# Stage C of a Fourier mix in products of 64 rows

## The chip, the cores and the metric

The kernel runs on one core of one Trainium2 chip. The metric is the time of one execution on the device in microseconds, as a median over several runs. TensorE multiplies, ScalarE (ACT) and VectorE (DVE) evacuate and combine, GpSimd (POOL) issues the loads, and SyncE (SP) issues most of the stores.

## The reference

The input `x` has 8 batches of 3072 rows and 256 columns. First the real part of a two-dimensional Fourier transform is taken, over the rows and the columns of each batch. Then follows a channel mix:

```
X = fft(fft(x, axis=1), axis=2).real
x_prev = X shifted by one row, zeros in front
xk = mu_k * X + (1 - mu_k) * x_prev
xr = mu_r * X + (1 - mu_r) * x_prev
k  = relu(xk @ w_k)              # 256 -> 1024
v  = (k * k) @ w_v               # 1024 -> 256
out = sigmoid(xr @ w_r) * v
```

## The kernel before

**Stages.** The transform of one batch goes through three stages of products on TensorE. Stage A (`a_item`, for the first two batches in part `a_sum`) transforms along one part of the row index. Stage D (`d_item`, L502) transforms the 256 columns and leaves its result in `g_all`: 13 units `u` of 256 columns on 128 partitions, the lower 64 of which belong to one value of the remaining row index and the upper 64 to another. `turned` (L524) corrects one column of each unit by a small product of 13 columns. Stage C (`c_item`, L527 to L543) finishes the row transform, for 27 slots of 64 rows of the result. For slot `sl` the weights are a unit `u` of `g_all`, of the first 128 columns (`f` = 0, giving p) or the second (`f` = 1, giving q), and the moving operand is `m_cs[:, f, sl]`, 64 columns. An odd slot needs only the lower 64 partitions of its unit and an even slot only the upper 64; `m_cs` has zeros in the other half, so that one product over all 128 partitions and 128 columns computes two neighbouring slots (192 columns and three slots for the first, which shares its unit). The products of an item go to one PSUM buffer, p in its first bank and q in the second, and ScalarE copies both to the tile `pq` (`evac`, L443). `halves` (L547 to L557) then forms p + q and p - q on VectorE into `y`; `diff`, `scaled` and `mixed` make the differences of neighbouring rows and the two mixed inputs out of it.

**Channel mix.** The rows of a batch are six chunks of 512. For each chunk there are four steps. In each, `k_piece` makes four products of 512 columns (L625) into a PSUM buffer, ScalarE takes the Relu (L635), and VectorE squares it later (L642). `v_tile` multiplies the squares of an earlier chunk with `w_v` in eight products of 256 columns (L663), five steps behind. Once for each chunk `r_item` makes eight products of 256 columns (L649), and ScalarE takes their sigmoid.

**Order.** The order of all work is written out by hand. A step is: `k_piece`, then the items that the dictionary `work` holds for the step as kind "x" (stages A, D and C, `turned`, `r_item`), then `v_tile`, then kind "w" (VectorE's parts and the loads), then the output and the squares. A batch has 24 steps, and while batch b is mixed, batches b+1 and b+2 go through the transform. Stage C of batch t = b+2 stands at steps 24b+35, 37, 39 and 41 (that is, 11, 13, 15 and 17 of the next batch), with 7, 8, 6 and 6 slots; that of batch 1 at steps 16 to 19. `halves` of a batch stands at steps 16 and 18 of the batch before it (17 and 20 for batch 1). `pin_order` keeps each engine's instructions in the order in which they are written.

**PSUM.** The large buffers (`ps_w`, 1024 columns of float32, two banks) are three in rotation; `k_piece`, the "x" items and `r_item` share them. Two small ones (`ps_v`) serve `v_tile`. A product that takes a buffer waits until its last reader is done.

Batch 0's stage C uses `c_item` in smaller pieces, some of them with an extra product one column wide (`turn_late`), and is not changed but for the layout of `pq`.

Of the kernel before, what the change touches and what calls it, by code (L numbers as in the profile page):

```python
# [10 lines left out]
FP16 = mybir.dt.float16  # L11
# [9 lines left out]
def _v(ap, extra_offset, free_dims):  # L21
    new_ap = [list(ap.ap[0])] + [[s, c] for (s, c) in free_dims]
    return dataclasses.replace(ap, offset=ap.offset + extra_offset, ap=new_ap)
# [16 lines left out]
def kernel(  # L40
# [10 lines left out]
    nc = tc.nc  # L51
# [3 lines left out]
    P = 128  # L55
    N1, R = 48, 64
    NSL = 27
    NU = 26
    NJ, NJ1, NJ2 = 14, 6, 9
# [5 lines left out]
    y_pool = ctx.enter_context(tc.tile_pool(name="y_sb", bufs=1))  # L65
# [8 lines left out]
    def ps_slot(kind, n, cols):  # L74
        k = ps_n[kind] % n
        ps_n[kind] += 1
        return psum.tile([P, cols], FP32, name=f"ps{kind}{k}", tag=f"ps{kind}{k}", bufs=1)

    def ps_w():
        return ps_slot("W", 3, 1024)  # L80

    def ps_v():
        return ps_slot("V", 2, 512)
# [23 lines left out]
    V = nc.vector  # L107
# [122 lines left out]
    g_all = const.tile([P, NU // 2, 256], FP16)  # L230
# [3 lines left out]
    m_cs = const.tile([P, 2, 2 * NJ, 64], FP16)  # L234
# [125 lines left out]
    ps = ps_v()  # L360
    for a in range(2):
        nc.tensor.matmul(out=ps[:, 2 * a:2 * a + 2], lhsT=mu_p[:, a], rhs=unit, start=True,
                         stop=True)
# [73 lines left out]
    y_t = {}  # L437

    def evac(out_ap, in_ap, eng):
        if eng == "V":  # L440
            V.tensor_copy(out=out_ap, in_=in_ap)
        else:
            nc.scalar.activation(out=out_ap, in_=in_ap, func=AF.Copy)  # L443
# [83 lines left out]
    def c_item(b, s0, n, eng="A", turn_late=False, small=False):  # L527

        if s0 == 0:
            y_t[b] = y_pool.tile([P, 2, NSL, 64], FP16, name="y")  # L530
            y_t[b, "pq"] = y_pool.tile([P, 2, NSL, 64], FP16, name="pq")
        pq = y_t[b, "pq"]
        ps, bank = (ps_v(), 256) if small else (ps_w(), 512)
        cuts = [s0] + list(range(s0 + (1 + s0 % 2 if s0 else 3), s0 + n, 2))
        for f in range(3 if turn_late else 2):
            for sl in cuts:
                k = min(1 + sl % 2 if sl else 3, s0 + n - sl)
                o, u = bank * min(f, 1) + 64 * (sl - s0), max(sl - 1, 0) // 2
                m = 1 if f == 2 else P
                nc.tensor.matmul(out=ps[0:m, o:o + 64 * k],  # L540
                                 lhsT=g_all[:, u, 128 * min(f, 1):128 * min(f, 1) + m],
                                 rhs=m_cs[:, f % 2, sl:sl + k], start=True, stop=True)
        evac(pq[:, :, s0:s0 + n, :], _v(ps, 0, [(bank, 2), (64, n), (1, 64)]), eng)  # L543


    x_t = {}
# [1 line left out]
    def halves(b, lo, hi, hs=(0, 1)):  # L548

        pq = y_t[b, "pq"]  # L550
        if b and (lo, hs[0]) == (0, 0):

            V.tensor_scalar(out=pq[0:1, 1, 0], in0=pq[0:1, 1, 0], scalar1=-1.0, scalar2=None,
                            op0=ALU.mult)
        for h in hs:
            V.tensor_tensor(out=y_t[b][:, h, lo:hi], in0=pq[:, 0, lo:hi], in1=pq[:, 1, lo:hi],  # L556
                            op=ALU.subtract if h else ALU.add)  # L557

    def diff(b, lo, hi, hs=(0, 1)):
# [150 lines left out]
    ps = ps_w()  # L710
    for u, eng in ((4, "A"), (6, "V")):
        d_half(0, u, ps[:, 256 * u - 1024:256 * u - 512], eng)
    c_item(0, 0, 5, "A", True)
    c_item(0, 5, 4, "A", True)
    c_item(0, 9, 4, "A", True, True)
    c_item(0, 13, 4, "A", True, True)

    work = {}  # L720

    def at(step, f, *args):
        work.setdefault((step, "x" if f in (a_item, a_sum, d_item, c_item, turned, r_item) else "w"),
                        []).append((f, args))

    def mirrored_mu():
# [12 lines left out]
    for step, (c, tb) in v_steps.items():  # L739
        if c == chunks[-1] and tb >= 2:  # L740
            o_steps[step] = [(c, tb, 1)]
        elif tb % 2:
            o_steps[step + (step == LAG)] = [(c, tb, 2)]
    halves(0, 0, 5)
    diff(0, 0, 4)
    mix_part(0, 0, 0, 4)
    halves(0, 5, 9)
    keep_busy(20, ps_w(), 128)
    k_products(chunks[0], 0, 0, 256)
# [3 lines left out]
    for n, c in enumerate(chunks):  # L753
        at(4 * n + (4, 5, 6)[(n < 3) + (n == 0)], r_item, c)


    at(0, halves, 0, 9, 17)
    at(0, diff, 0, 8, 16)
    at(0, mix_part, 0, 0, 8, 16)
    at(4, loads_2)  # L760
# [30 lines left out]
    for n, st0 in enumerate((11, 12, 13, 14)):  # L791
        at(st0, d_item, 1, n)
    at(15, turned, 0, 13)
    for n, st0 in enumerate((16, 17, 18, 19)):
        at(st0, c_item, 1, (0, 7, 15, 21)[n], (7, 8, 6, 6)[n])

    for b in range(B):
        s0 = 24 * b

        for n, st0 in enumerate((2, 4, 6, 8) if b else ()):  # L800
            at(s0 + st0, mix, b, n // 2, 1, n % 2)
        if b + 3 < B:
            for h in range(2):
                at(s0 + 12 + 2 * h, load_xh, b + 3, h)
        t = b + 2
        if t < B:
            for n, st0 in enumerate((9, 10, 12, 14) if b else (13, 15, 16, 24)):
                at(s0 + st0, butterfly if n % 2 else fold, t, n // 2)
            for n, st0 in enumerate((18, 21, 23, 25) if b else (18, 21, 25, 26)):
                at(s0 + st0, a_item, t, n // 2, n % 2)  # L810
            for n, st0 in enumerate((27, 29, 31, 33)):
                at(s0 + st0, d_item, t, n)
            at(s0 + 34, turned, 0, 13)
            for n, st0 in enumerate((35, 37, 39, 41)):
                at(s0 + st0, c_item, t, (0, 7, 15, 21)[n], (7, 8, 6, 6)[n])
        t = b + 1
        if t < B:
            at(s0 + (16 if b else 17), halves, t, 0, 15)
            at(s0 + (18 if b else 20), halves, t, 15, 27)
            at(s0 + (19 if b else 20), diff, t, 0, 26, (0,))  # L820
            at(s0 + (20 if b else 22), diff, t, 0, 26, (1,))
            at(s0 + 21, mix, t, 0, 0, 0)
            at(s0 + 22, mix, t, 0, 0, 1)
            at(s0 + 24, mix, t, 1, 0, 0)
            at(s0 + 25, mix, t, 1, 0, 1)
# [51 lines left out]
```

## Time and profile before

| | |
|---|---|
| median of 3 runs | 444.59 us (444.22 to 444.69) |
| the profiled execution | 443.51 us, span 441.7 us |
| granted clock of TensorE | 1.00 |
| TensorE busy | 431.9 us, 98% |
| VectorE busy | 361.0 us, 82% |
| ScalarE busy | 326.7 us, 74% |
| stage C's products (L540) | 216, of which 34 in batch 0 |

Lines of the profile name a source line, an engine, an operation and the tiles: `PE L540 MATMUL psW<-m_cs,g_all 128*128 128x128 f16 x8` are eight products at L540, with weights of 128 rows and 128 columns (128*128) and a moving operand of 128 rows and 128 columns. PE are the products, PEld the weight loads, each of which is an instruction of its own. In a timeline the first number is the start and the second the time covered, in us from the start of the span; neighbouring instructions of one kind are merged. Products are pipelined: a product lasts longer than the distance to the next one, and that distance is what it costs.

### The profile page before, as it was taken

Reading aid. Unit: us, or ns where it says so; the run is one execution under the profiler, and the core shown is the slowest. Engines: PE = TensorE matmul, PEld = TensorE weight load, DVE = VectorE, ACT = ScalarE, POOL = GpSimd, SP = SyncE. Lnnn points to the kernel's source line nnn. Section 1 sums busy time; section 2 is a strip of 40 time slices with the busy share of each in tenths; the row PEclk is TensorE's granted clock in tenths of the full one; section 3 lists DMA queues with packets and bytes.
Section 4 is the critical chain, followed back from the end, with each engine's and each line's share of the span. In section 5 each row is a group of like instructions: output and inputs, shape, how many; then the busy total and the mean of one; then the engine's idle time right before and its main releaser. Section 6 shows DMA issues by size and latency. Waiting matters only on the chain.

```text
span 441.7 us, 8525 instructions
## 1 busy us (share of the span) xinstructions
PE 431.9 (98%) x3484; PEld 309.4 (70%) x3484; DVE 361.0 (82%) x532; ACT 326.7 (74%) x377; POOL 50.9 (12%) x66
## 2 busy tenths in 40 slices
PE   9889999999999999999999999999999999999995
PEld 3657776777777777777777777777777777676764
DVE  7699999988798978978799887989789756997553
ACT  8669887877777777787777777777777877666661
POOL 7763030004000120002200010000000000000000
PEclk9999999999999999999999999999999999999999
DMA  7998676239523492326723273232322223233334
GB/s 126 182 207 129 134 132 140 57 68 162 128 53 73 77 193 61 64 60 114 171 48 73 54 138 71 51 73 48 73 60 62 63 57 72 49 73 72 73 73 95
DMA packets 34507, 40.93 MB, mean 93 GB/s; under 512 B 3906, under 2 KB 30788, under 8 KB 34468
## 3 DMA queue, kind: packets, MB, share of 16 engines
q1 hardware_dynamic: 27524, 25.05, 25.3%
q0 software_dynamic: 6784, 15.21, 21.3%
q8 instruction: 27, 0.44, 0.4%
q10 hardware_dynamic: 160, 0.13, 0.1%
q14 instruction: 12, 0.10, 0.1%
HBM read 30.41 MB, written 25.17 MB: 126 GB/s over the span
## 4 chain that ended last, share of the span: by engine, by line
PE 86%; DVE 5%; DMA 4%; POOL 2%; issue 1%; ACT 1%; POOLq 0%
PE psV L663 36%; PE psW L625 35%; PE psW L649 9%; DMA xp<-in_x_dram 2%; PE psW L502 2%; PE psW L540 2%; PE psW L463 2%; DMA wr<-in_moe_w_r_dram,row_i 2%; DVE k L642 1%; POOL xm L125 1%; DVE x L589 1%; POOL wk L125 1%; DVE d L564 1%; DVE p L153 1%; DVE t L576 1%
## 5 line engine op out<-in xcount | busy, mean ns | idle before, releaser
L635 ACT ACTIVATE rl<-psW 128x1024 f16<-128x1024 f32 x192 | 196.4, 1024 | 101.5 <-PE psW L625 97.6
L663 PE MATMUL psV<-wv_sb,k 128*128 128x256 f16 x1536 | 198.9, 273 | 0.3 <-DVE k L642 0.3
L625 PE MATMUL psW<-x,wk 128*128 128x512 f16 (+1 forms) x776 | 197.3, 377 | 1.9 <-ACT rl L635 0.8
L663 PEld LDWEIGHTS <-k 128*128 128x128 f16 x1536 | 146.1, 98 | 28.5 <-DVE k L642 0.6
L642 DVE TENSOR_TENSOR k<-rl 128x2048 f16<-128x2048 f16 (+1 forms) x98 | 117.6, 1201 | 50.5 <-ACT rl L635 50.2
L625 PEld LDWEIGHTS <-wk 128*128 128x128 f16 x776 | 75.9, 98 | 52.1 <-issue 2.8
L673 DVE SCALAR_TENSOR_TENSOR o<-psV,r 128x512 f32<-128x512 f32 (+1 forms) x97 | 66.1, 682 | 16.1 <-PE psV L663 13.7
L589 DVE TENSOR_TENSOR x<-y,t 128x1536 f16<-128x1536 f16 (+1 forms) x70 | 61.8, 882 | 2.4
L649 PE MATMUL psW<-wr,x 128*128 128x256 f16 x384 | 49.8, 273 | 0.0
L654 ACT ACTIVATE r<-psW 128x1024 f16<-128x1024 f32 x48 | 48.9, 1018 | 0.8 <-PE psW L649 0.8
L649 PEld LDWEIGHTS <-x 128*128 128x128 f16 x384 | 37.6, 98 | 14.6 <-issue 0.3
L125 POOL DMA_INDIRECT xm<-in_x_dram,idx x25 | 31.3, 1250 | 8.1 <-issue 6.9
L122 POOL DMA_DIRECT2D xp<-in_x_dram x16 | 9.1, 567 | 192.6 <-DVE p L155 184.5
L443 ACT ACTIVATE pq<-psW 128x768 f16<-128x768 f32 (+5 forms) x32 | 27.4, 858 | 1.0 <-PE psW L540 1.0
L443 ACT ACTIVATE g_all<-psW 128x1024 f16<-128x1024 f32 (+4 forms) x39 | 27.7, 712 | 0.0
L443 ACT ACTIVATE a<-psW 128x832 f16<-128x832 f32 x30 | 25.8, 859 | 1.8 <-PE psW L480 1.8
L153 DVE TENSOR_TENSOR p<-xp,xm 96x2304 f16<-96x2304 f16 (+3 forms) x19 | 20.9, 1101 | 0.0
L576 DVE TENSOR_SCALAR t<-d,mu_f 128x1536 f16<-128x1536 f16 (+1 forms) x38 | 20.6, 542 | 0.1
L540 PEld LDWEIGHTS <-g_all 128*128 128x128 f16 (+1 forms) x216 | 14.9, 97 | 7.7
L502 PEld LDWEIGHTS <-a 128*128 128x128 f16 x208 | 14.1, 98 | 8.2 <-issue 1.2
L576 DVE TENSOR_SCALAR t<-d,mu_m 128x1536 f16<-128x1536 f16 x32 | 19.7, 615 | 0.0
L556 DVE TENSOR_TENSOR y<-pq 128x960 f16<-128x960 f16 (+5 forms) x38 | 18.6, 532 | 1.0 <-ACT pq L443 0.8
(99 smaller groups left out, 182.7 us busy)
## 6 DMA issues: line engine op xcount, KB each, us to landing
out_dram<-o SPq DMA_DIRECT2D x190, 128.0 KB, 2.4
xp<-in_x_dram POOLq DMA_DIRECT2D x8, 432.0 KB, 6.6
xp<-in_x_dram POOLq DMA_DIRECT2D x8, 384.0 KB, 4.7
wv_sb<-in_moe_w_v_dram POOLq DMA_DIRECT2D x1, 512.0 KB, 8.3
xm<-in_x_dram,idx POOLq DMA_INDIRECT x25, 7.3
out_dram<-o ACTq DMA_DIRECT2D x2, 64.0 KB, 2.1
out_dram<-o SPq DMA_DIRECT2D x2, 64.0 KB, 2.2
wk<-in_moe_w_k_dram,row_i POOLq DMA_INDIRECT x4, 7.1
```

The source lines that it names most:

```text
L125: nc.gpsimd.indirect_dma_start(dst, None, src, bass.IndirectOffsetOnAxis(ap=idx, axis=0))
L153: V.tensor_tensor(out=p[:, q0:q0 + n], in0=xp[:, q0:q0 + n], in1=_v(xm, o + 256, [(-256, n), (-1, 256)]), op=ALU.add)
L443: nc.scalar.activation(out=out_ap, in_=in_ap, func=AF.Copy)
L576: V.tensor_scalar(out=dst, in0=src, scalar1=mu, scalar2=None, op0=ALU.mult)
L589: V.tensor_tensor(out=dst, in0=_v(y_t[b], 64 * (NSL * a + lo + 3 * m), [(1, n)]), in1=_v(x_t["t", a], 64 * lo, [(1, n)]), op=ALU.subtract ...
L625: nc.tensor.matmul(out=st["k", ds][:, 512 * hs + lo:512 * hs + hi], lhsT=wk_sb[m][a][:, 128 * fc:128 * fc + 128], rhs=xk[:, a, 512 * i + l ...
L635: nc.scalar.activation(out=st["rl"][:, 2 * ds:2 * ds + 2], in_=st["k", ds].rearrange("p (f t) -> p f t", f=2), func=AF.Relu, bias=0.0, sca ...
L642: V.tensor_tensor(out=k2_t[c][:, lo:hi], in0=r, in1=r, op=ALU.mult)
L649: nc.tensor.matmul(out=ps[:, 256 * tb:256 * tb + 256], lhsT=x_t[b, 1, m][:, a, 512 * i + 128 * tb: 512 * i + 128 * tb + 128], rhs=wr_sb[m] ...
L654: nc.scalar.activation(out=st["r", c], in_=ps, func=AF.Sigmoid)
L663: nc.tensor.matmul(out=st["v", tb - h][:, 256 * h:256 * h + 256], lhsT=k2_t[c][:, fc, 128 * tb:128 * tb + 128], rhs=wv_sb[:, fc], start=(f ...
L673: V.scalar_tensor_tensor(out=o.rearrange("p a b -> p (a b)")[:, 0:256 * n], in0=st["v", t0][:, 0:256 * n], scalar=16.0, in1=st["r", c][:, ...
```

## The change

Stage C of batches 1 to 7 goes through a new function, `c_pairs`. For each slot it uses only the 64 partitions that the slot needs: rows 0 to 63 of `g_all` and `m_cs` for an odd slot, rows 64 to 127 for an even one. Every slot is then two products of 64 rows, 64 moving columns and 128 weight columns (p and q), each with its own weight load. The products alternate between an odd and an even slot, and the two write to different banks of the PSUM buffer. 28 slots are computed, one more than is used. The items are four of 8, 8, 8 and 4 slots, two and two in one step: steps 16, 16, 19, 19 for batch 1, and 24b+36, 36, 39, 39 for the others. The tile `pq` is laid out by slot and then p or q, so that an evacuation writes runs of 128 elements, and `halves` reads runs of 64 with gaps of 64.

```diff
         if s0 == 0:
             y_t[b] = y_pool.tile([P, 2, NSL, 64], FP16, name="y")
-            y_t[b, "pq"] = y_pool.tile([P, 2, NSL, 64], FP16, name="pq")
+            y_t[b, "pq"] = y_pool.tile([P, 2 * NJ, 2, 64], FP16, name="pq")
...
-        evac(pq[:, :, s0:s0 + n, :], _v(ps, 0, [(bank, 2), (64, n), (1, 64)]), eng)
+        evac(_v(pq, 128 * s0, [(64, 2), (128, n), (1, 64)]),
+             _v(ps, 0, [(bank, 2), (64, n), (1, 64)]), eng)
+
+    def c_pairs(b, s0, n):
+        if s0 == 0:
+            y_t[b] = y_pool.tile([P, 2, NSL, 64], FP16, name="y")
+            y_t[b, "pq"] = y_pool.tile([P, 2 * NJ, 2, 64], FP16, name="pq")
+        ps = ps_w()
+        for i in range(n // 2):
+            for f in range(2):
+                for odd in (1, 0):
+                    sl = s0 + 2 * i + odd
+                    o, u = 512 * odd + 128 * i + 64 * f, min(max(sl - 1, 0) // 2, NU // 2 - 1)
+                    rows = slice(0, 64) if odd else slice(64, 128)
+                    nc.tensor.matmul(out=ps[:, o:o + 64],
+                                     lhsT=g_all[rows, u, 128 * f:128 * f + 128],
+                                     rhs=m_cs[rows, f, sl], start=True, stop=True)
+        evac(_v(y_t[b, "pq"], 128 * s0, [(256, n // 2), (128, 2), (1, 128)]),
+             _v(ps, 0, [(128, n // 2), (512, 2), (1, 128)]), "A")
...
-            V.tensor_scalar(out=pq[0:1, 1, 0], in0=pq[0:1, 1, 0], scalar1=-1.0, scalar2=None,
+            V.tensor_scalar(out=pq[0:1, 0, 1], in0=pq[0:1, 0, 1], scalar1=-1.0, scalar2=None,
                             op0=ALU.mult)
         for h in hs:
-            V.tensor_tensor(out=y_t[b][:, h, lo:hi], in0=pq[:, 0, lo:hi], in1=pq[:, 1, lo:hi],
+            V.tensor_tensor(out=y_t[b][:, h, lo:hi], in0=pq[:, lo:hi, 0], in1=pq[:, lo:hi, 1],
                             op=ALU.subtract if h else ALU.add)
...
-        work.setdefault((step, "x" if f in (a_item, a_sum, d_item, c_item, turned, r_item) else "w"),
+        work.setdefault((step, "x" if f in (a_item, a_sum, d_item, c_item, c_pairs, turned, r_item) else "w"),
                         []).append((f, args))
...
-    for n, st0 in enumerate((16, 17, 18, 19)):
-        at(st0, c_item, 1, (0, 7, 15, 21)[n], (7, 8, 6, 6)[n])
+    for n, st0 in enumerate((16, 16, 19, 19)):
+        at(st0, c_pairs, 1, 8 * n, (8, 8, 8, 4)[n])
...
-            for n, st0 in enumerate((35, 37, 39, 41)):
-                at(s0 + st0, c_item, t, (0, 7, 15, 21)[n], (7, 8, 6, 6)[n])
+            for n, st0 in enumerate((36, 36, 39, 39)):
+                at(s0 + st0, c_pairs, t, 8 * n, (8, 8, 8, 4)[n])
```

## The prediction

> **What bounds the kernel now.** I read the page's busy line first, then the chain that ended last, then the timeline of one stretch of the steady state, and last the timeline where TensorE changes between shapes of different height or width.
>
> ```profile
> PE 431.9 (98%) x3484; PEld 309.4 (70%) x3484; DVE 361.0 (82%) x532; ACT 326.7 (74%) x377; POOL 50.9 (12%) x66
> ...
> PE 86%; DVE 5%; DMA 4%; POOL 2%; issue 1%; ACT 1%; POOLq 0%
> ...
> L540 PEld LDWEIGHTS <-g_all 128*128 128x128 f16 (+1 forms) x216 | 14.9, 97 | 7.7
> ```
>
> TensorE is busy for 98% of the span and is 86% of the chain; stage C (L540) is a small part of it. The timeline says what a product costs when the next one follows at once (ACT's lines in it are used further on):
>
> ```profile
> 151.27 0.19 PE L524 MATMUL psW<-g_all,turn 128*128 128x13 f16 x1
> 151.30 1.03 PE L663 MATMUL psV<-wv_sb,k 128*128 128x256 f16 x8
> ...
> 153.03 0.55 PE L540 MATMUL psW<-m_cs,g_all 128*128 128x192 f16 x6
> ...
> 153.42 1.04 PE L663 MATMUL psV<-wv_sb,k 128*128 128x256 f16 x8
> ...
> 154.29 1.03 PE L625 MATMUL psW<-x,wk 128*128 128x512 f16 x4
> ...
> 155.16 1.04 PE L649 MATMUL psW<-wr,x 128*128 128x256 f16 x8
> 155.36 1.02 ACT L635 ACTIVATE rl<-psW 128x1024 f16<-128x1024 f32 x1 [0.29 <-PE psW L625]
> ...
> 156.90 1.03 PE L625 MATMUL psW<-x,wk 128*128 128x512 f16 x4
> ...
> 157.77 0.61 PE L540 MATMUL psW<-m_cs,g_all 128*128 128x128 f16 x8
> ...
> 158.21 1.04 PE L663 MATMUL psV<-wv_sb,k 128*128 128x256 f16 x8
> ```
>
> Starts, not durations, are to be read. Four products of 512 columns take 156.90 to 157.77, 217 ns each; eight of 128 take 157.77 to 158.21, 55 ns each. Each has a weight load of its own, and it is hidden. The straight line through the two sizes is 0.42 ns a column and gives 28 ns for 64 columns. The product of 13 columns took 30 ns (151.27 to 151.30), where the line says 7. So a product and its load, on the same rows, do not follow closer than some 30 ns.
>
> Entering and leaving another tile shape is in two views of the start, products first, weight loads second:
>
> ```profile
> 25.53 0.27 PE L625 MATMUL psW<-x,wk 128*128 128x256 f16 x1
> 25.73 0.17 PE L301 MATMUL psW<-rw 1*128 1x1 f16 x1
> ```
> ```profile
> 25.42 0.10 PEld L625 LDWEIGHTS <-wk 128*128 128x128 f16 x1
> 25.73 0.11 PEld L301 LDWEIGHTS <-rw 1*128 1x128 f16 x2 [0.21 <-issue]
> 25.86 0.10 PEld L625 LDWEIGHTS <-wk 128*128 128x128 f16 x1
> ```
>
> A 256-column product is followed after 0.11 us elsewhere (153.42 to 154.29 for eight). Before a product of one row it takes 0.20 us (25.53 to 25.73), and the load is not pulled ahead: 0.09 us more. On the way back, the second one-row product began at about 25.77 (the two end at 25.93, and one lasts 0.16), and the next load of full height at 25.86, 0.09 us later against some 0.03: 0.06 us more. The same drain stands at a change of width:
>
> ```profile
> 20.65 0.22 PE L540 MATMUL psW<-m_cs,g_all 128*1 128x128 f16 x1
> 20.80 0.29 PE L540 MATMUL psV<-m_cs,g_all 128*128 128x128 f16 x2
> ```
>
> A product of 128 columns, then 0.15 us to the next start where 55 ns is usual: 0.095 us more.
>
> **The change, part by part.**
>
> *Removed.* Stage C of one batch is 26 products of 128 rows in four items. By the timeline, the first item takes 153.03 to 153.42 and the second 157.77 to 158.21; the two of six products take 6 x 55 ns each. 0.39 + 0.44 + 0.33 + 0.33 = 1.49 us for a batch.
>
> *Added products.* 28 slots in two products each are 56 products of 64 columns, every one with its own load. No row shows two products on different halves of the rows side by side. By the nearest rows on each side, 28 ns (line) and 30 ns (13 columns), I take 29 ns: 56 x 29 = 1.62 us, 0.13 us more than before. Bound below: the halves overlap fully and a pair takes 29 ns, 0.81 us, 0.68 us less. Bound above: in this mode a load is no longer hidden by the product before it, 28 + 29 = 57 ns each, 3.19 us, 1.70 us more. I take the middle because every row has a load in each spacing, and none goes under that floor.
>
> *Added changes of height.* The items stand two and two in a step, so TensorE goes to 64 rows and back twice in a batch. Each group costs 0.09 in and 0.06 to 0.095 out, 0.15 to 0.19; two are 0.30 to 0.38, and I take 0.35 us. Nothing covers it, since TensorE is the bound; it would be nothing only if 64 rows counted as the same shape as 128, as 96 rows do (L463 follows L625 without a gap).
>
> *Sum for a batch:* 0.13 + 0.35 = +0.48 us on TensorE.
>
> *Which batches pay.* The seven behind the first are changed. For batches 2 to 7 TensorE runs without a gap around stage C, so 6 x 0.48 = 2.9 us reach the end. Batch 1 is different: its halves, differences and mixes (L556 to L589) end late on VectorE, and TensorE waits for them:
>
> ```profile
> 75.88 0.96 DVE L589 TENSOR_TENSOR x<-y,t 128x1536 f16<-128x1536 f16 x1
> 76.04 0.38 PE L625 MATMUL psW<-x,wk 128*128 128x512 f16 x1
> ...
> 76.89 0.81 PE L625 MATMUL psW<-x,wk 128*128 128x512 f16 x3 [0.47 <-DVE x L589]
> ```
>
> From 76.04 the next product is due at 76.26 and starts at 76.89: 0.63 us of slack. An extra 0.48 us is swallowed there if VectorE's chain stays where it is. Batch 1 counts 0, between -0.3 (its last halves come earlier) and +0.48.
>
> *Evacuations.* ScalarE now copies 1024 + 1024 + 1024 + 512 columns instead of 896 + 1024 + 768 + 768. By the page's rows, 3 x 1.02 + 0.59 = 3.65 us instead of 0.91 + 1.02 + 0.81 + 0.81 = 3.55. ScalarE idles for a quarter of the span, so the 0.1 us is hidden. What is new is their place: two in one step, behind the Relu and, in the first of the two steps, a Sigmoid. Let T be the start of that step's 512-column products. The second item takes the PSUM buffer of that step's own Relu. The stretch from 154.29 has the Relu start 1.07 us after T (155.36) and end at T + 2.09. The K products end their turn at T + 0.87, R's at T + 1.74, the drain makes it 1.83, and the first item's 16 products end at T + 2.30. So the buffer is free 0.2 us early. ScalarE then works to T + 5.15, the next Relu starts some 0.35 us late, and nobody needs it soon: its products are used by V five steps after the chunk began. The second step has no Sigmoid and room left. Cost 0; if the products overlapped, the buffer would be 0.05 us late.
>
> *VectorE.* The halves now read p and q in runs of 64 with gaps. Nearest row: the butterfly reads runs of 128 with gaps and takes 680 ns for 1024 elements, against 685 for the contiguous square of 1024. I take 0. The other end is the rate of the copy out of PSUM, 691 ns for 512 (1.35 ns an element instead of 0.7): some 2.2 us a batch, hidden by VectorE's idle 18%, but for batch 1 it would lie on the path. No DMA is moved or passed; the halves keep their steps, and what they wait for is ready one or two steps earlier.
>
> **Sum.** The profiled execution took 443.51 us (span 441.7), 1.08 below the median of 444.59. 443.51 + 2.9 = 446.4 us; on the median, 447.5 us. Own range of this case: 28 ns and 0.30 give +2.3, seven batches at 30 ns and 0.38 give +4.0, so 446.9 to 448.6.
>
> **The rivals.**
>
> *The halves overlap (faster).* If the load and the product on one half run beside those on the other, a pair takes 29 ns, and a batch 0.81 + 0.35 - 1.49 = -0.33 us. Six batches give -2.0, and seven -2.3: 442.3 to 442.6; with the late buffer 442.8. I give 442.6. It decides below 41 ns a pair, since 28 x 41 + 350 ns is 1.49 us. Against it: no two starts with loads in the trace are closer than some 30 ns. For it: in all those rows load and product share their rows, so the floor may belong to one set of rows and not to the queue. By the Trainium skill, "TensorE: Matmul & The Clock Gate", part 3 on packing small matmuls, products on different row groups start some 4 ns apart, and a load overlaps a product in flight where the row group differs; that is this rival, and no run so far shows it.
>
> *Half an overlap.* A pair of 38 to 45 ns leaves a batch within 0.12 us of before: 444 to 445.4. No row speaks for it.
>
> *Loads exposed.* 57 ns for every product: +1.70 + 0.35 = 2.05 us a batch, 7 x 2.05 - 0.63 = +13.7, 458 us. For it: after a change of shape the load was not pulled ahead. Against it: the two one-row loads began 0.02 us apart (0.11 us for two of 0.09). If the loads are exposed but the halves overlap, a pair takes 57 ns, which is the forecast again.
>
> *The change does nothing on the path* would need TensorE to have slack at stage C; of the late batches none has.
>
> **How the numbers follow.** Forecast 0.50, halves overlap 0.36, half an overlap 0.06, loads exposed 0.08. A measurement tells about 0.2% (0.9 us) from no change. Faster: 0.37 (overlap, and a little of the half). Same: 0.06. Slower: 0.57. The range 442.3 to 448.6 takes in forecast and overlap; outside are the exposed loads and an overlap that is better than 29 ns a pair.
>
> **What would show it.** Right: starts of the 64-column products some 29 ns apart, or in twos 57 ns apart; 0.09 us before the first and after the last of each group; the gap at 76 us shorter by some 0.5 us. Wrong: pairs that follow after 30 ns, groups without a gap at their ends, the L556 rows longer, or TensorE waiting for a Relu in the second item.

## The result and the profile after

The changed kernel takes 442.86 us (median, 442.19 to 443.21), the one before 444.22 us (seven runs of each): a ratio of 0.9968, with a 95% interval of 0.9956 to 0.9980. It is faster by 1.36 us, where 3 us slower was forecast. In two later comparisons it came out at 0.9968 (0.9946 to 0.9990) and 0.9970 (0.9960 to 0.9981).

The busy line of the page after, and the chain:

```profile
PE 430.6 (98%) x3694; PEld 304.8 (69%) x3694; DVE 360.4 (82%) x532; ACT 326.1 (74%) x377; POOL 48.5 (11%) x66
...
PE 90%; DVE 6%; ACT 1%; DMA 1%; issue 1%
```

TensorE is the bound as before and is busy 1.3 us less, with 210 more products. The timeline of TensorE at the two groups of one batch shows where that comes from:

```profile
154.42 1.04 PE L670 MATMUL psW<-wr,x 128*128 128x256 f16 x8
155.39 0.72 PE L560 MATMUL psW<-m_cs,g_all 64*128 64x64 f16 x32
156.03 0.61 PE L684 MATMUL psV<-wv_sb,k 128*128 128x256 f16 x4
```
```profile
160.82 0.59 PE L646 MATMUL psW<-x,wk 128*128 128x512 f16 x2
161.35 0.52 PE L560 MATMUL psW<-m_cs,g_all 64*128 64x64 f16 x24
161.81 0.39 PE L684 MATMUL psV<-wv_sb,k 128*128 128x256 f16 x2
```

Read the starts. 24 products of 64 columns and their way out take 161.35 to 161.81, 0.46 us, or 19 ns each with everything in it. At 29 ns each the products alone would have taken 0.70 us. A window that ends some 15 ns into the first group has two products in it, which together last as long as one:

```profile
155.39 0.20 PE L560 MATMUL psW<-m_cs,g_all 64*128 64x64 f16 x2
```

Start by start, the trace gives this for the second group (ns from one start to the next):

```
4 35 3 26 3 26 3 26 4 25 4 26 3 26 3 26 3 26 3 26 4 25 4
```

Two products start 3 to 4 ns apart, and the next two 29 ns after them. The weight loads come in twos in the same way, 3 to 4 ns apart. The two halves run side by side, loads included. By the Trainium skill, "TensorE: Matmul & The Clock Gate", part 3, products on different row groups start some 4 ns apart; the trace agrees, with 3 to 4. In the second item of the first group, which starts behind a wait, the two of a pair start 6 to 20 ns apart, and still two come in every 29 ns.

The changes of height are there too. From the last 256-column product to the first of 64 rows it is 205 ns instead of 109, and from a 512-column one 311 instead of 216 (0.095 us more). From the last of 64 rows to the next product it is 122 ns instead of 29 (0.093 us more), and that next product itself is followed after 120 ns instead of 109 (0.011 us more). In the first group there is a third loss: 89 ns instead of 26 between the two items. ScalarE's timeline names it:

```profile
154.62 1.02 ACT L656 ACTIVATE rl<-psW 128x1024 f16<-128x1024 f32 x1 [0.71 <-PE psW L646]
155.54 1.02 ACT L675 ACTIVATE r<-psW 128x1024 f16<-128x1024 f32 x1
```

The Relu ends at 155.64, and the second item, which takes its PSUM buffer, begins at 155.69.

From the product before a group to the product after it, less what the product before takes itself, the groups cost 0.744 and 0.551 us in every batch; with the 0.011 us behind each they come to 1.317 us together. Before, stage C cost 1.505 us, measured in the same way. That is 0.19 us less a batch. The distance from `turned` in one batch to `turned` in the next says the same: 51.28 us instead of 51.47 for every batch from the second on. For batches 2 to 7 it makes 1.12 us. Batch 1 has the gap in front of it:

```profile
75.71 0.96 DVE L610 TENSOR_TENSOR x<-y,t 128x1536 f16<-128x1536 f16 x1
...
75.83 0.38 PE L646 MATMUL psW<-x,wk 128*128 128x512 f16 x1
...
76.72 0.59 PE L646 MATMUL psW<-x,wk 128*128 128x512 f16 x2 [0.51 <-DVE x L610]
```

TensorE arrives 0.21 us earlier (75.83, before 76.04) and goes on 0.17 us earlier (76.72, before 76.89), since VectorE's mix ends earlier. 1.12 + 0.17 = 1.29 us, which is the difference of the two spans (441.7 and 440.4 us); the medians differ by 1.36. VectorE's halves cost what they did:

```profile
L577 DVE TENSOR_TENSOR y<-pq 128x960 f16<-128x960 f16 x14 | 8.6, 656 | 0.3
...
L577 DVE TENSOR_TENSOR y<-pq 128x768 f16<-128x768 f16 x14 | 7.2, 553 | 0.2 <-ACT pq L443 0.2
```

656 and 553 ns stand against 655 and 552 before: runs of 64 with gaps cost next to nothing.

### The profile page after: what moved, and what is told of

It is laid out like the page before. It is cut to its first block, busy times and chain, and to the rows that moved or that the text cites. A ratio compares the mean times of both kernels' runs of the same rounds, so it can differ in the third digit from the quotient of the medians.

```text
span 440.4 us, 8945 instructions
## 1 busy us (share of the span) xinstructions
PE 430.6 (98%) x3694; PEld 304.8 (69%) x3694; DVE 360.4 (82%) x532; ACT 326.1 (74%) x377; POOL 48.5 (11%) x66
## 4 chain that ended last, share of the span: by engine, by line
PE 90%; DVE 6%; ACT 1%; DMA 1%; issue 1%
PE psV L684 37%; PE psW L646 35%; PE psW L670 9%; PE psW L502 2%; PE psW L463 2%; PE psW L185 2%; PE psW L560 2%; DVE k L663 1%; DMA xp<-in_x_dram 1%; DVE d L585 1%; DVE x L610 1%; DVE p L153 1%; DVE t L597 1%; PE psV L301 1%; DVE y L577 1%
## 5 line engine op out<-in xcount | busy, mean ns | idle before, releaser
L646 PE MATMUL psW<-x,wk 128*128 128x512 f16 (+1 forms) x776 | 197.3, 377 | 1.9 <-ACT rl L656 0.8
L646 PEld LDWEIGHTS <-wk 128*128 128x128 f16 x776 | 75.9, 98 | 52.1 <-issue 2.8
L125 POOL DMA_INDIRECT xm<-in_x_dram,idx x25 | 28.5, 1140 | 8.1 <-issue 6.9
L443 ACT ACTIVATE pq<-psW 128x1024 f16<-128x1024 f32 (+3 forms) x32 | 26.8, 892 | 1.0 <-PE psW L540 1.0
L163 DVE TENSOR_TENSOR eo<-p 96x1024 f16<-96x1024 f16 (+2 forms) x28 | 17.8, 676 | 0.0
```

What stands on the lines that cost most here:

```text
L125: nc.gpsimd.indirect_dma_start(dst, None, src, bass.IndirectOffsetOnAxis(ap=idx, axis=0))
L646: nc.tensor.matmul(out=st["k", ds][:, 512 * hs + lo:512 * hs + hi], lhsT=wk_sb[m][a][:, 128 * fc:128 * fc + 128], rhs=xk[:, a, 512 * i + l ...
```

## The experiments

The theory after the result: loads and products of one half run beside those of the other, and each half by itself keeps the 29 ns of before. The rivals: a product of 64 rows is cheaper in any order; or the gain lies in the steps and the evacuations. The first four of these kernels ran on one chip.

**Neighbours on the same half.**

```diff
-        for i in range(n // 2):
-            for f in range(2):
-                for odd in (1, 0):
+        for odd in (1, 0):
+            for i in range(n // 2):
+                for f in range(2):
...
```

> The changed kernel, but within each item all products of the lower 64 rows come first and then all of the upper 64, so neighbours share a half. Theory (a load and a product on one half run beside those on the other half, and each half by itself keeps the old floor of some 29 ns): starts 28 to 30 ns apart, 56 x 29 = 1.64 us a batch, plus 0.38 for four changes of height, less the 1.50 of before: +0.5 us a batch, six batches count, +3.1 us on the kernel before, ratio 1.007. Rival (a product of 64 rows is itself cheaper, in whatever order, for instance because a load of half the height takes half the time): starts some 15 ns apart as in the changed kernel, ratio 0.997.

Measured: 444.38 us beside 444.28, ratio 1.0004 (0.9995 to 1.0013). Neither number came. The first group of one batch in the timeline, and the distances between the starts in it (ns, the first 18):

```profile
155.73 0.83 PE L560 MATMUL psW<-m_cs,g_all 64*128 64x64 f16 x32
156.49 0.39 PE L684 MATMUL psV<-wv_sb,k 128*128 128x256 f16 x2
```
```
38 29 29 30 8 21 18 10 19 11 18 30 29 16 13 15 14 14
```

The 29 ns are there, wherever one half is alone: that part of the theory holds, and the rival of the cheap product falls (it would show 15 throughout). But after the fifth product the gaps come in twos that sum to 29 again. The item has eight products of the lower half first. Three of them had not started when, by the pattern, the first of the upper half did (the last section has a record that shows the order directly). So the two halves overlapped for a part of each item although the program did not alternate, and the groups cost 0.860 + 0.684 = 1.544 us. With 0.011 us behind each that is 0.06 us a batch more than before, or +0.4 us for batches 2 to 7, inside the measured interval (-0.2 to +0.6 us). The expectation had left out that products of one half can pass waiting ones of the other.

**The steps and the layout alone.** The products of 128 rows of before, at the new steps and with the new layout of `pq`:

```diff
             for n, st0 in enumerate((36, 36, 39, 39)):
-                at(s0 + st0, c_pairs, t, 8 * n, (8, 8, 8, 4)[n])
+                at(s0 + st0, c_item, t, (0, 7, 15, 21)[n], (7, 8, 6, 6)[n])
```

(and batch 1 likewise at 16, 16, 19, 19)

> The changed kernel with its steps (16, 16, 19, 19 and 36, 36, 39, 39) and its layout of p and q, but the products of 128 rows of before. Theory (the gain is in the products): no more than batch 1's earlier chain, 0 to -0.2 us, ratio 1.000. Rival (the gain comes from where the items stand and how they are evacuated): ratio 0.997 or below.

Measured: 444.20 us, ratio 0.9999 (0.9990 to 1.0008). A batch takes 51.48 us in this trace, against 51.47 before. The gain is not in the placement or the layout; it is in the products. The evacuations of this run are not quite those of the changed kernel (they write runs of 64, not of 128), so it does not test them alone; but the starts on TensorE already account for all of the 0.19 us a batch.

**Four visits in a batch instead of two.**

```diff
-    for n, st0 in enumerate((16, 16, 19, 19)):
+    for n, st0 in enumerate((16, 17, 18, 19)):
...
-            for n, st0 in enumerate((36, 36, 39, 39)):
+            for n, st0 in enumerate((35, 37, 39, 41)):
```

> The changed kernel with one item in a step: 16, 17, 18, 19 for batch 1 and 24b+35, 37, 39, 41 for the others, so TensorE goes to 64 rows and back four times in a batch instead of two. Theory (each visit costs 0.19 us, nothing covers it): two more visits a batch, less the 0.06 us that the second item waited: +0.32 us a batch, six to seven batches, +1.9 to +2.2 us on the changed kernel, ratio to the kernel before 1.001 to 1.002. Rival (the drain is paid once for the pair spacing, or a shorter stay saves it elsewhere): ratio 0.997.

Measured: 445.42 us, ratio 1.0025 (1.0014 to 1.0035), slower than before. Against the changed kernel's 0.9968 that is 0.0057, or 2.5 us, where 1.9 to 2.2 were expected. One of its visits, then its shortest one:

```profile
154.60 0.41 PE L560 MATMUL psW<-m_cs,g_all 64*128 64x64 f16 x16
154.94 0.50 PE L684 MATMUL psV<-wv_sb,k 128*128 128x256 f16 x3
```
```profile
168.10 0.29 PE L560 MATMUL psW<-m_cs,g_all 64*128 64x64 f16 x8
168.33 0.50 PE L684 MATMUL psV<-wv_sb,k 128*128 128x256 f16 x3
```

The pairs are as close as in the changed kernel, but each visit pays 0.095 us in, 0.093 out and 0.011 on the product behind. The four cost 3 x 0.435 + 0.319 + 4 x 0.011 = 1.668 us a batch, 0.16 more than the 128-row products and 0.35 more than two visits; batch 1 pays the 0.35 too, and 7 x 0.35 is the 2.5 us. The drain (the time that TensorE loses between products of one height and of the other) is real, it adds up by visits, and it decides the sign: with two visits the change gains 0.19 us a batch, with four it loses 0.16.

**The first group one step later.** Step 24b+37 has no R item, so its own products and the two items are all that take the three PSUM buffers:

```diff
-            for n, st0 in enumerate((36, 36, 39, 39)):
+            for n, st0 in enumerate((37, 37, 39, 39)):
```

> The changed kernel with the first two items of batches 2 to 7 one step later, at 24b+37, which has no R item and no Sigmoid, so that the second item finds a PSUM buffer free. Theory (the 89 ns between the two items, against 26 elsewhere, is a wait for that step's Relu): no such gap in batches 2 to 7, 6 x 0.06 = 0.4 us less than the changed kernel, ratio to before 0.996. Rival (the gap belongs to the border between two items, or the wait moves to the next Relu or Sigmoid): gap or a new one of the same size, ratio 0.997.

Measured: 442.59 us, ratio 0.9956 (0.9943 to 0.9970). Its first group:

```profile
157.90 0.64 PE L560 MATMUL psW<-m_cs,g_all 64*128 64x64 f16 x32
158.47 0.39 PE L684 MATMUL psV<-wv_sb,k 128*128 128x256 f16 x2
```

157.90 to 158.47 is 0.57 us, where the changed kernel has 0.64 (155.39 to 156.03). The gap of 89 ns is gone in batches 2 to 7 and still there in batch 1, which was left at its step. The groups cost 0.668 + 0.552 = 1.220 us. So the gap was the wait for the Relu. The interval of the time overlaps the changed kernel's; the trace is clearer than the time: a batch takes 51.21 us instead of 51.28.

**A whole group by halves.** To test the passing, with the same later step:

```diff
...
+        items = [(s0, 8), (s0 + 8, n - 8)]
+        pss = [ps_w() for _ in items]
+        for odd in (1, 0):
+            for ps, (z, m) in zip(pss, items):
+                for i in range(m // 2):
+                    for f in range(2):
+                        sl = z + 2 * i + odd
...
-            for n, st0 in enumerate((36, 36, 39, 39)):
-                at(s0 + st0, c_pairs, t, 8 * n, (8, 8, 8, 4)[n])
+            for n, st0 in enumerate((37, 39)):
+                at(s0 + st0, c_pairs, t, 16 * n, (16, 12)[n])
```

> The changed kernel with the first group at 24b+37 for batches 2 to 7, and within a whole group of two items all products of the lower half first and then all of the upper half (16 and 16, then 12 and 12). The run with the halves in turn by item had a look-ahead: the first upper product began when three lower ones had not. Theory (each half keeps 29 ns, and products of the other half may pass some three that wait): the upper half begins 8 ns after the 13th lower product of 16, and after the 9th of 12, so the groups take 1.03 and 0.80 us from the end of the product before to the next 128-row product: 1.83 us a batch instead of 1.50 before, six to seven batches, +2.0 to +2.3 us on before, ratio 1.005. Rival (products keep their order, and the earlier run's overlap was something else): 1.12 and 0.87 us, +0.49 us a batch, ratio 1.007. Rival (the look-ahead grows with what is queued): under 1.6 us a batch, ratio 1.001 or less.

Measured: 452.34 us beside 448.79, ratio 1.0079 (1.0052 to 1.0106). The chip of this comparison was slower for every kernel, the kernel before too, so only ratios on it compare. Two groups of batch 2:

```profile
109.40 1.00 PE L562 MATMUL psW<-m_cs,g_all 64*128 64x64 f16 x32
110.33 0.39 PE L687 MATMUL psV<-wv_sb,k 128*128 128x256 f16 x2
```
```profile
113.92 0.77 PE L562 MATMUL psW<-m_cs,g_all 64*128 64x64 f16 x24
114.62 0.28 PE L687 MATMUL psV<-wv_sb,k 128*128 128x256 f16 x1
```

In the first, the gaps are 29 ns up to the 13th product, then 9, and after the overlap of a few products 29 again to the end. In the second, the short gap stands after the 9th of 12. The groups cost 1.033 and 0.799 us; 1.03 and 0.80 were expected from a look-ahead of three products, 1.12 and 0.87 without one. The look-ahead does not grow with the group. The time rose by more than the 0.5% expected; taken alone it would fit the rival without passing (1.007) better, and it is the group times that decide against that rival. Part of the excess is in the trace: two second groups had a wait of 0.6 and 0.06 us between their items. The rest was not followed up.

The run also bears on a rival that was not named. In the changed kernel the lower half writes one PSUM bank and the upper half the other, so two neighbours differ in bank as well as in half. Here the 8th and the 9th product of a group are of the same half and go to two different buffers, and so to different banks; they start 30 and 29 ns apart in the two groups. Another bank alone does not let two products overlap. Whether two halves would overlap in one bank is shown by no run.

**The better step again, beside the changed kernel.** The two kernels were run side by side twice more, the second time with a version whose second group stands at 24b+41.

> The changed kernel itself, beside the others on one chip: ratio 0.997.

> The changed kernel with the first two items of batches 2 to 7 at 24b+37, beside the changed kernel on one chip: 0.4 us less than it, ratio 0.996.

On the slower chip: 0.9968 (0.9946 to 0.9990) for the changed kernel and 0.9968 (0.9946 to 0.9989) for the later step (medians 447.39 and 447.81 us), no gain of one over the other. In this profile the later step's first groups were as short as before (0.67 us), but in batches 2 to 4 the second group waited 0.2 to 0.4 us between its items for the Relu of the step before, because ScalarE had begun a copy of the first group late:

```profile
215.52 1.02 ACT L443 ACTIVATE pq<-psW 128x1024 f16<-128x1024 f32 x1
...
217.33 1.02 ACT L443 ACTIVATE pq<-psW 128x1024 f16<-128x1024 f32 x1 [0.79 <-PE psW L646]
...
219.32 0.29 PE L560 MATMUL psW<-m_cs,g_all 64*128 64x64 f16 x8 [0.26 <-ACT rl L656]
```

The second copy started 0.79 us after the first had ended, although its products were done by 215.2. The profile puts the wait down to products at L646, which the copy does not read; why it waited is open.

> The changed kernel itself, beside the next two on one chip: ratio 0.997, and 89 ns between the two items of the first group in every batch.

> The first group of batches 2 to 7 at 24b+37, the second at 24b+39 as in the changed kernel. If its gain of 0.4 us is real: ratio 0.996, groups of 0.67 and 0.55 us. If the waits that one of its two profiles showed in the second group (0.2 to 0.45 us in batches 2 to 4) come often: second groups over 0.7 us and a ratio no better than the changed kernel's.

> The first group of batches 2 to 7 at 24b+37 and the second at 24b+41, so that two more steps lie between them and ScalarE is done with the first group's copies when the second takes its PSUM buffers. If closeness of the groups made those waits: groups of 0.67 and 0.55 us in every batch, ratio 0.996 or a little below. If not: the same waits, or VectorE's last halves late, since they stand one step behind; ratio 0.997 or above.

On the third occasion the changed kernel had 442.98 us, 0.9970 (0.9960 to 0.9981); the later step 442.51, 0.9957 (0.9943 to 0.9970); the groups further apart 442.49, 0.9963 (0.9949 to 0.9976). Both later versions had groups of 0.67 and 0.55 us in batches 2 to 7, and no wait in the second. So the later step is worth some 0.4 us by the trace (6 x 0.075 us). The medians agree in two comparisons of three, with intervals that overlap, and show nothing on the slower chip; setting the groups further apart adds nothing that can be told.

## Why the prediction was wrong

*Bound:* right. TensorE had no slack at stage C in batches 2 to 7, and what was saved there came out at the end (with batch 1, 1.29 us by the trace, 1.36 measured).

*Added products:* this is the step that failed. I took 29 ns for each product; the runs show 29 ns for each pair, 0.82 us a batch instead of 1.62. The number was right for one half, as the run with neighbours on the same half shows. It was carried over to two halves by the row that was nearest in size, and in every such row load and product shared their rows. The text of the rival had said so, and yet I gave it 0.36. The likelier case should have been chosen by asking what the rows have in common with the new form. They had the size in common and not the thing that was new, so they bore on the price of one half and not on the overlap.

*Changes of height:* close, 0.20 us a group against 0.15 to 0.19; 0.40 a batch against 0.35. The 0.011 us on the product behind a group had not been seen. This was the term that mattered most: twice as many visits turn the gain into a loss.

*The wait for the buffer:* said to be 0 in the forecast and 0.05 us with overlap, where its own terms (2.09 less 1.83 and 8 x 0.029) give 0.03; it was 0.063 us, in the place described.

*Batch 1:* counted 0; it gave 0.17 us, within its bounds. Its gap did not shrink, because TensorE and VectorE's chain both came earlier.

*Evacuations and VectorE:* 0, and nothing was seen.

*The rival that came true* had -0.33 us a batch; it was -0.19. The difference is the two changes of height (0.05 more), the wait (0.06), and some 0.04 at the ends of the groups: the second pair follows after 39 ns instead of 29, and the last product starts 4 to 20 ns after its neighbour. Against that, the products taken out had cost 1.505 us and not 1.49. Its time of 442.6 was 0.3 us too low.

## What to carry to other kernels

A price taken from the nearest row holds for what the row shares with the new form; where the new form is there to share a resource that no row shares, the overlap is to be priced apart, with its own chance. Products on half the rows are worth it only if many stand together: a visit costs 0.20 us here and a pair of 64-column products saves 56 - 29 = 27 ns against one 128-row product of 128 columns, so a visit has to hold more than seven pairs. In the run with four visits, those of eight pairs cost 0.446 us and eight such 128-row products 0.447 before: eight only break even. And a group that takes several PSUM buffers in one step is best put where no other item wants them.

## What the runs showed of the hardware that was not expected

Products of the two halves need not be written in turn to overlap. With eight, twelve or sixteen of one half first, the other half began when three of the first were still waiting, and the two then ran side by side. The records do not name the half; the reading rests on the gaps, on the first product of each half lasting some 200 ns instead of 190, and on the group times of 1.03 and 0.80 us that were worked out from it beforehand. One pair of records shows it directly. The first product of an item carries the wait for its PSUM buffer and the last one the signal that the item is done, and the trace marks both. In the run with neighbours on the same half, the first product of the second item, the 17th of its group in the program, started before the last of the first item, the 16th, in all 14 groups: at 306 and 348 ns from the start of the group that is shown. It also means that starts are in the order of the program within a half, and not across the two.
